# Two gated attentions on one core: the last score group in three parts

## The chip, the cores and the metric

The kernel runs on one core of a Trainium2 chip. The metric is the device time of one execution in microseconds (us), lower is better. Before the change three executions took 889.76, 890.76 and 892.24 us; the median is 890.76. The engines of the core are named as in the profile: PE (TensorE, matrix products), ACT (ScalarE, activation functions), DVE (VectorE), POOL (GpSimd) and SP (SyncE, which here issues DMAs). Scores and sums are accumulated in PSUM, eight banks of 128 x 512 floats.

## The reference

Both branches read the same input of 2048 rows and 640 columns, with 32 heads of 20 columns. Branch A is full softmax attention; branch B looks back over 8 positions with a distance of 2. A sigmoid gate mixes them.

```python
def _A_ref(x, wqkv, wo):                       # B, S, D = 1, 2048, 640; H = 32; Dh = 20
    qkv = (x @ wqkv).reshape(B, S, 3, H, Dh).transpose(2, 0, 3, 1, 4)
    q, k, v = qkv[0], qkv[1], qkv[2]
    scores = jnp.einsum("bhqd,bhkd->bhqk", q, k) * Dh ** -0.5
    p = _softmax(scores, axis=-1)
    o = jnp.einsum("bhqk,bhkd->bhqd", p, v)
    return o.transpose(0, 2, 1, 3).reshape(B, S, D) @ wo
# _B_ref: the same with keys and values of positions s, s-2, ..., s-14 only
g = _sigmoid((x * gate_w).sum(-1, keepdims=True))
return g * _A_ref(x, A_wqkv, A_wo) + (1 - g) * _B_ref(x, B_wqkv, B_wo)
```

## The kernel before, in words

**Groups and units.** Branch A's scores are cut into 32 groups: a chunk of 512 queries (`qc`, four of them) and a quad of four heads (`q`, eight of them), in the order of the list `GO` (line 37). A unit is one head j of the quad and one block of 128 keys against the 512 queries: a product of 128 x 512 scores, 64 units to a group. `HG` is the number of the last group. Before the change it is already cut in two halves of 256 queries (`GX`, line 41), and a unit of it then holds two key blocks of 256 queries each, so that it still fills one bank with 512 columns. In all there are 2048 units.

**Steps.** The program goes in steps that alternate between three and two units (`ST`, line 289: banks 0 to 2 and banks 3 and 4). In a step, PE computes the scores into the banks (`mk_qk`, lines 1258 and 1261), and ACT takes one exponential over all of them (`mk_exp`, line 1306) into one of six buffers `ebuf`. PE later multiplies these by V (`mk_pv`, line 1337) and adds them up in bank 5 (`OB`), which all groups share. Banks 6 and 7 serve all other products.

**Units on VectorE.** Some units get their exponential from VectorE, in pairs: a first step from PSUM for each (line 1489), then four passes over the pair (lines 1509, 1512, 1515, 1522) that form the exponential by a polynomial, into a buffer `xo`. Such a unit uses bank 6 or 7 (`gen_xm`), or takes the third bank of a three-unit step (`xstep`), whose exponential on ACT then covers two units. `xpick` chooses the group; `XMIN`, `XLAST` and `XAHEAD` say how much of a group must still be left, and `X0` is the first step from which it is allowed.

**Normalization.** When a group's products with V are complete, `gen_norm` lets VectorE transpose bank 5 into `rg` (line 723), take reciprocals of the sums (726), multiply by the gate (728), scale (733) and transpose back into `oTn` (736). Only when the first transpose has read bank 5 may the next group's products go there.

**The output.** For the first three chunks `gen_fold` multiplies both branches by their output weights and stores 128-row blocks. For the last chunk, `gen_prefold` does all of branch B and the first five quads (`NPF`) of branch A for its four blocks ahead of time. Blocks 0 and 1 are kept as floats (`accin`, line 803); blocks 2 and 3 as a high and a low bf16 part (`acch`, lines 795 and 798), to be brought back into PSUM by two products with the identity (line 844). After the first half of the last group is normalized (`oTh` 0), `gen_lfold` adds the last three quads of blocks 0 and 1 and stores them from SP, beside the exponentials. For blocks 2 and 3, `gen_l3` and `last_pre2` put the stored parts and two of the last quads into four banks, and `last_end` adds the last quad (four matmuls), copies block 3 on VectorE (line 885) and block 2 on ACT (line 883), and stores each with one DMA (line 815).

**What sets the order.** All instructions are laid down when the program is built. A planner (`_Sched` and the main loop from line 1890) keeps a clock for each engine with fixed costs for each instruction, for exponentials

```python
ED = {3: 1330.0, 2: 903.0, 1: 480.0}
```

in ns for three, two and one unit. Work other than scores stands in lanes, Python generators that offer their next instruction; `turns` ranks them, and `ready` lets one go when its inputs and its engine would be free. Between steps the planner fills PE's time with products with V, with lane work, or with spare products (`spare`) where PE's share of the last 3.4 us would fall under `SPW`. `SEG` (line 1865) gives another set of these parameters for each stretch of 24 steps; stretches that it does not name get `BASE`. The real engines follow the order of their own lists and wait on semaphores for each other.

Of the kernel before, what the change touches and what calls it, by code (L numbers as in the profile page):

```python
# [10 lines left out]
ALU = mybir.AluOpType  # L11
# [3 lines left out]
P = 128  # L15
S = 2048
D = 640
# [23 lines left out]
GX = GO + [(QCN, LQ)]  # L41
GI[(QCN, LQ)] = len(GO)
QL = [n for n, g in enumerate(GO) if n == 0 or GO[n - 1][1] != g[1]]
# [234 lines left out]
def _build(ctx, nc, A_x, A_wqkv, A_wo, B_wqkv, B_wo, gate_w, out):  # L278
# [97 lines left out]
    acch = [qk[:, o * D:(o + 2) * D].rearrange("p (i h k) -> p i h k", i=2, h=2) for o in (4, 6)]  # L376
# [339 lines left out]
    def gen_norm(gi):  # L716
# [3 lines left out]
        n, o = (512, 0) if gi < HG else (256, 256 * (gi - HG))  # L720
# [4 lines left out]
        yield ("dve", 240.0, 0.0)  # L725
        T("dve", lambda e: e.reciprocal(rr[i][:, 0:m], rg[i][:, 0:n:32]), reads=["rg"], writes=[("rr", i)], cost=150.0 + 6 * m)
        yield ("dve", 180.0, 0.0)
# [4 lines left out]
        yield ("dve", 500.0, 0.0)  # L732
        T("dve", lambda e: e.tensor_tensor(rgn[i][:, 0:m, 1:1 + DH], rg_v, rr_b, ALU.mult),
          reads=["rg", ("rr", i)], writes=["rgn"], cost=170.0 + 21 * m)
        yield ("dve", 710.0, 0.0)
        T("dve", lambda e: e.transpose(oTn[:, sl, o:o + n], rgn[i][:, 0:m, :]), reads=["rgn"],
          writes=[("oTn", sl)] if gi < HG else [("oTn", sl), ("oTh", 0)] if gi == HG else [("oTh", 1)], cost=180.0 + n * 1.04)
# [43 lines left out]
    def gen_prefold(qc):  # L781
# [3 lines left out]
        for blk in range(4):  # L785
            for hf in range(2):
# [5 lines left out]
                if blk >= 2:  # L792
                    ac = acch[blk - 2]
                    yield ("dve", 480.0, 0.0)
                    T("dve", lambda e, b=b, hf=hf, ac=ac: e.tensor_copy(ac[:, 0, hf, :], bank[b][:, 0:FW]),
                      reads=[("bk", b)], writes=[("acch", blk, 0, hf), "qB", "kB"], cost=480)
                    yield ("dve", 490.0, 0.0)
                    give(b, T("dve", lambda e, b=b, hf=hf, ac=ac: e.tensor_tensor(ac[:, 1, hf, :], bank[b][:, 0:FW], ac[:, 0, hf, :],
                                                                                 ALU.subtract),
                              reads=[("bk", b), ("acch", blk, 0, hf)], writes=[("acch", blk, 1, hf), "qB", "kB"], cost=490))  # L800
                    continue
# [5 lines left out]
    def a_half(o, blk, hf, qs, rds, first, last, b):  # L807
        for q in qs:
            st, sp = first and q == qs[0], last and q == qs[-1]
            T("pe", lambda e, q=q, st=st, sp=sp: e.matmul(o, *a_mm(o, QCN - 1, q, blk, FW * hf)[1:], start=st, stop=sp),  # L810
              reads=[("oTh", blk // 2) if q == LQ else ("oTn", ((QCN - 1) * NQUAD + q) % NOT)] + [("woA_r", q, j) for j in range(4)],
              **({"writes": [("bk", b)]} if st else {"accum": [("bk", b)]}), cost=140)
# [24 lines left out]
    def l_banks(blk):  # L837
        x = ST[NS_[0] % 2][0]
        return (x, x + 1) if blk == 2 else (6, 7)

    def l_pre(blk, hf, k):
        b = l_banks(blk)[hf]
        if k < 2:
            T("pe", lambda e: e.matmul(bank[b][:, 0:FW], ident[:, :], acch[blk - 2][:, k, hf, :], start=(k == 0), stop=False),
              reads=["ident", ("acch", blk, k, hf)], **({"accum": [("bk", b)]} if k else {"writes": [("bk", b)]}), cost=140)
        else:
            a_half(bank[b][:, 0:FW], blk, hf, [NPF + k - 2], None, False, False, b)

    LP = NQUAD - 1 - NPF + 2

    def gen_l3():
        for hf in range(2):
            while not (pre.done and xmlane.done and normdone.get(HG - 1) and (hf == 0 or lfl.done)):
                yield ("poll",)
            b = yield from take(True, 6 + hf)
            for k in range(LP):
                yield ("pe", 140.0, 1.0)
                l_pre(3, hf, k)
            bst[b] = None
            unch()  # L860

    l2done = [False]

    def last_pre2(s):
        if not l2done[0] and pre.done and normdone.get(HG - 1) and all(x[0] == s - 1 for x in pend):
            l2done[0] = True
            for hf in range(2):
                for k in range(LP):
                    l_pre(2, hf, k)

    def last_end():
        for blk in (3, 2):
            for hf in range(2):
                b = l_banks(blk)[hf]
                a_half(bank[b][:, 0:FW], blk, hf, [LQ], None, False, True, b)
        for blk in (3, 2):
            b = l_banks(blk)[0]
            o_ap = outl[:, blk, :].rearrange("p (h k) -> p h k", h=2)
            i_ap = ps[:, b * 512:(b + 2) * 512].rearrange("p (h k) -> p h k", h=2)[:, :, 0:FW]
            rd = [("bk", b) for b in l_banks(blk)]  # L880
            wr = [("outl", blk, 0), ("outl", blk, 1)]
            if blk == 2:
                T("act", lambda e, o_ap=o_ap, i_ap=i_ap: e.activation(o_ap, i_ap, ACTF.Copy), reads=rd, writes=wr, cost=700)
            else:
                T("dve", lambda e, o_ap=o_ap, i_ap=i_ap: e.tensor_copy(o_ap, i_ap), reads=rd, writes=wr, cost=780)
            out_blk("act" if blk == 2 else "sp", blk)
# [362 lines left out]
    GROUPS = QCN * NQUAD + 1  # L1249
    left = [[GX[g] + (kb, j) for kb in range(KBN if g < HG else KBN // 2) for j in range(4)] for g in range(GROUPS)]  # L1250
    n0 = [len(l) for l in left]

    def qk_mm(e, o, un):
# [5 lines left out]
        h = 256 * (g - HG)  # L1259
        for i in range(2):  # L1260
            ins = e.matmul(o[:, 256 * i:256 * i + 256], kT[js, q, (2 * kb + i) * P:(2 * kb + i + 1) * P], qT[HG % NQT][js, h:h + 256],
                           start=True, stop=True)
# [5 lines left out]
    def kbs(un):  # L1268
        return [un[2]] if GI[un[0:2]] < HG else [2 * un[2], 2 * un[2] + 1]
# [47 lines left out]
    def mk_pv(us):  # L1317
# [10 lines left out]
        def fn(e):  # L1328
            ins = None
            for (key, ap, un), (st, sp) in zip(seq, flags):  # L1330
# [4 lines left out]
                o = 256 * (g - HG) if g >= HG else 0  # L1335
# [23 lines left out]
    def xpick():  # L1359
# [14 lines left out]
    XLAST = 24  # L1374
# [286 lines left out]
    lane(gen_l3(), "l3", gstep(20))  # L1661
# [156 lines left out]
    def turns(s):  # L1818
        act = [g for g in lanes if not g.done and s >= g.s0]
        act.sort(key=lambda g: (not (g.hold or (g.name[:4] == "norm" and int(g.name[4:]) not in obrd)), 0 if g.name == "pre" or g.name[0] == "O" and odl[g.name] - s < ODM else RANK.get(g.name[0], 0), g.dl))  # L1820
# [4 lines left out]
        if xlane.hold and PX:  # L1825
            n = sum(1 for g in act if g.hold or (g.name[:4] == "norm" and int(g.name[4:]) not in obrd))
# [26 lines left out]
    def to(s, t, lim):  # L1853
        while clk["dve"] < t:
# [10 lines left out]
    SEG = {0: (0.68, 150.0, 28, 20, 40, 12, 300000.0, 0, 1000.0, 1, 0.85, 20, 3000.0, 1000000000.0),  # L1865
# [128 lines left out]
```

## Time and profile before

| | |
|---|---|
| median of three executions | 890.76 us |
| the profiled execution: time, span of its instructions | 891.71 us, 889.9 us |
| ACT busy | 873.4 us (98%) |
| VectorE busy, TensorE busy | 821.0 us (92%), 823.0 us (92%) |
| exponentials on ACT | 779 instructions: 338 of three units, 441 of two |
| first exponential starts | 18.52 us |
| mean granted TensorE clock | 0.997 |

In the lines of the groups a row gives the source line, the engine, the operation, the tile written and the tile read, their shapes and the count, then the busy time in us and the mean duration of one in ns, and then the idle time of the engine in front of them with what ended it. Exponentials overlap a little on ACT, so their mean durations add up to more than the busy time. The timeline gives the start, the duration of a merged stretch, and in brackets the idle time ahead of it. The chain is followed back from the last instruction to what released each step. A row by windows gives, for each engine in the order PE, PEld (weight loads), DVE, ACT, POOL, its busy time and its instructions, then the granted TensorE clock, the busy share of the DMA engines and the GB/s that they moved.

### The profile page before, as it was taken

What the parts mean: (1) busy time and instruction counts of PE and PEld (TensorE: products, weight loads), DVE (VectorE), ACT (ScalarE), POOL (GpSimd) and SP (SyncE); (2) the same over time, 40 slices, a digit from 0 to 9 for tenths busy, and PEclk for the clock granted to TensorE, in tenths of its full rate; (3) what the DMA queues carried; (4) which work ended last, traced back from release to release, by engine and by line L of the source; (5) the groups of instructions that cost most, each with busy time, mean ns of one, the idle gap of its engine ahead of it and who ended that gap; (6) DMA issues with size and microseconds to landing.
All of it is one profiled execution on the core that took longest, in us unless ns stands there. A gap on an engine that the chain in (4) does not pass through costs nothing.

```text
span 889.9 us, 16166 instructions
## 1 busy us (share of the span) xinstructions
PE 823.0 (92%) x6702; PEld 257.4 (29%) x6702; DVE 821.0 (92%) x1178; ACT 873.4 (98%) x805; POOL 90.6 (10%) x111
## 2 busy tenths in 40 slices
PE   8999999999999999899998899999998999988897
PEld 6322332223233222222232222233322223322233
DVE  6499999999999999998889999999999999999995
ACT  6999999999999999999999999999999999999996
POOL 2000000000000012210001132001222000232100
PEclk9999999999999999999999999999999999999999
DMA  7232102011111447562113488204466300676300
GB/s 180 42 70 44 13 3 31 1 9 7 14 13 14 90 76 117 94 111 39 17 13 55 79 151 142 32 9 74 81 95 105 53 9 12 106 108 107 58 1 31
DMA packets 141005, 51.27 MB, mean 58 GB/s; under 512 B 120452, under 2 KB 128644, under 8 KB 140932
## 3 DMA queue, kind: packets, MB, share of 16 engines
q0 software_dynamic: 13824, 31.46, 20.9%
q1 hardware_dynamic: 126308, 18.51, 13.6%
q8 instruction: 53, 0.87, 0.4%
q10 hardware_dynamic: 800, 0.27, 0.1%
q14 instruction: 20, 0.16, 0.1%
HBM read 16.14 MB, written 2.62 MB: 21 GB/s over the span
## 4 chain that ended last, share of the span: by engine, by line
ACT 93%; PE 2%; DVE 2%; DMA 1%; issue 1%; SPq 0%; POOL 0%; DVEq 0%
ACT ebuf L1306 93%; DMA xT<-xT 1%; DMA x_tm<-in_A_x_dram 1%; PE ps L1169 0%; ACT L_sb L1037 0%; PE ps L1145 0%; DVE xI L1489 0%; PE ps L1258 0%; DVE xT L1102 0%; DVE xo L1522 0%; DVE xH L1515 0%; PE ps L1337 0%; PE ps L1791 0%; DVE xT L1092 0%; PE ps L469 0%
## 5 line engine op out<-in xcount | busy, mean ns | idle before, releaser
L1306 ACT ACTIVATE ebuf<-ps 128x1024 bf16<-128x1024 f32 (+1 forms) x779 | 860.3, 1468 | 2.0 <-PE ps L1258 1.9
L1258 PE MATMUL ps<-qT,kT 32*128 32x512 bf16 x1984 | 305.0, 385 | 55.7 <-ACT ebuf L1306 47.4
L1337 PE MATMUL ps<-ebuf,vA 128*21 128x512 bf16 (+1 forms) x1952 | 181.9, 377 | 0.9 <-ACT ebuf L1306 0.4
L1258 PEld LDWEIGHTS ps<-qT,kT 32*128 32x128 bf16 x1984 | 74.6, 91 | 345.4 <-ACT ebuf L1306 313.9
L1489 DVE TENSOR_SCALAR xI<-ps 128x512 int32<-128x512 f32 x152 | 103.3, 685 | 21.7 <-PE ps L1258 18.0
L1522 DVE SCALAR_TENSOR_TENSOR xo<-xI,xH 128x1024 int16<-128x1024 int32 x76 | 92.5, 1217 | 0.6
L1512 DVE SCALAR_TENSOR_TENSOR xH<-xU 128x1024 f32<-128x1024 f32 x76 | 92.3, 1215 | 0.6
L1515 DVE SCALAR_TENSOR_TENSOR xH<-xH,xU 128x1024 f32<-128x1024 f32 x76 | 92.1, 1212 | 0.3
L1104 POOL DMA_DIRECT2D accW<-tmps x36 | 31.7, 975 | 576.0 <-DVE tmps L1102 544.5
L469 PE MATMUL ps<-xT,WqkB 128*128 128x512 bf16 x200 | 59.1, 383 | 0.8 <-DVE xI L1489 0.4
L1337 PEld LDWEIGHTS ps<-ebuf,vA 128*21 128x21 bf16 x1952 | 37.0, 90 | 64.1 <-issue 56.4
L1509 DVE TENSOR_SCALAR xU<-xI 128x1024 f32<-128x1024 uint16 x76 | 51.9, 682 | 0.6
L975 DVE TENSOR_TENSOR prod<-qk 128x1024 bf16<-128x1024 bf16 x80 | 52.3, 682 | 0.1
L469 PE MATMUL ps<-xT,WqP 128*128 128x512 bf16 x155 | 47.2, 385 | 0.5 <-DVE qk L938 0.5
L469 PE MATMUL ps<-woA_r,oTn 128*128 128x320 bf16 x232 | 45.0, 301 | 0.0
L469 PE MATMUL ps<-xT,accW 128*128 128x512 bf16 x140 | 42.3, 384 | 0.0
L1791 PE MATMUL ps<-xT,ident 128*128 128x512 bf16 x132 | 41.0, 388 | 0.8 <-DVE xI L1489 0.6
L1796 PE MATMUL ps<-ident,zt 128*128 128x512 bf16 x126 | 41.6, 385 | 0.0
L1102 DVE TENSOR_TENSOR tmps<-vB,attnT 128x1280 f32<-128x1280 bf16 x24 | 35.5, 1479 | 2.4 <-DMA accW<-tmps 2.3
L1102 DVE TENSOR_TENSOR xT<-vB,attnT 128x1280 f32<-128x1280 bf16 x24 | 35.5, 1480 | 1.1 <-DMA xT<-xT 1.1
L678 DVE TENSOR_SCALAR qT<-ps 128x512 bf16<-128x512 f32 x32 | 22.1, 690 | 11.1 <-PE ps L675 10.5
L469 PE MATMUL ps<-WvA,oBacc 128*128 128x320 bf16 x160 | 31.8, 302 | 0.0
(125 smaller groups left out, 718.4 us busy)
## 6 DMA issues: line engine op xcount, KB each, us to landing
accW<-tmps POOLq DMA_DIRECT2D x36, 320.0 KB, 4.2
accW<-xT POOLq DMA_DIRECT2D x24, 320.0 KB, 4.1
xT<-xT POOLq DMA_DIRECT2D x24, 320.0 KB, 4.4
WqkB<-in_B_wqkv_dram SPq DMA_DIRECT2D x40, 160.0 KB
xT<-tmps POOLq DMA_DIRECT2D x12, 320.0 KB, 4.4
WqP<-in_A_wqkv_dram SPq DMA_DIRECT2D x135, 20.0 KB
x_tm<-in_A_x_dram SPq DMA_DIRECT2D x8, 320.0 KB
out_dram<-outsb SPq DMA_DIRECT2D x24, 80.0 KB
```

The source lines that it names most:

```text
L469: ins = e.matmul(o, l, r, start=(k0 + k == 0), stop=(k0 + k == n - 1))
L975: t = T("dve", lambda e, r=r, q_ap=q_ap, k_ap=k_ap: e.tensor_tensor(prod[r][:, :, :], q_ap, k_ap, ALU.mult), reads=["qB", "kB"], writes=[( ...
L1102: T("dve", lambda e, vv=vv, av=av, m=m: e.tensor_tensor(tmp4[m], vv, av, ALU.mult), reads=["aT", "vB4"], writes=[("tmps", m)] + dead, cost ...
L1258: return e.matmul(o, kT[js, q, kb * P:(kb + 1) * P], qT[g % NQT][js, :], start=True, stop=True)
L1306: return T("act", lambda e: e.activation(ebuf[s % NEB][:, 0:512 * n], ps[:, b0 * 512:(b0 + n) * 512], ACTF.Exp, scale=LN2 / ONE), reads=[( ...
L1337: ins = e.matmul(bank[OB][32 * j:32 * j + DH + 1, o:o + w], vA[:, q, kb, VW * j:VW * j + DH + 1], ap[:, w * i:w * i + w], start=st and i = ...
L1489: r = T("dve", lambda e, b=b, i=i, sl=sl: e.tensor_scalar(xIb[sl][:, 512 * i:512 * i + 512].bitcast(I32), bank[b], XB, 0.0, op0=ALU.add, o ...
L1509: T("dve", lambda e, xi=xi: e.tensor_scalar(xU[:, :], xi[:, :].bitcast(U16)[:, 0:2048:2], XV[0], XV[1], op0=ALU.mult, op1=ALU.add), reads= ...
L1512: T("dve", lambda e: e.scalar_tensor_tensor(xH[:, :], xU[:, :], XC[0], xU[:, :], ALU.add, ALU.mult), reads=["xU"], writes=["xH"], cost=1220)
L1515: T("dve", lambda e: e.scalar_tensor_tensor(xH[:, :], xH[:, :], XC[1], xU[:, :], ALU.add, ALU.mult), reads=["xU"], writes=["xH"], cost=1220)
L1522: t = T("dve", lambda e, r=r, xi=xi: e.scalar_tensor_tensor(xo[r][:, :].bitcast(I16), xi[:, :].bitcast(I32), XC[2], xH[:, :], ALU.mult, AL ...
L1796: T("pe", lambda e: e.matmul(bank[OB], zt[:, :], ones4, start=False, stop=False, skip_group_check=True), reads=["ident", "zt"], accum=[("o ...
```

## The change

The last group is cut into parts of 256, 128 and 128 queries (`SUB`), so that there are 34 parts in place of 33. A unit of the two small parts holds four key blocks of 128 queries. The normalizations of these last parts run without a break on VectorE and come ahead of other lanes. Block 2 of the last chunk is now treated as blocks 0 and 1 were: kept as floats, completed by `gen_lfold` once the second part is normalized, and stored from SP beside the exponentials. Only block 3 is left for the end: its stored parts are put into the two banks of the step that would come next, and `last_end` adds the last quad with two matmuls, copies one half on ACT and the other on VectorE, and stores each half with a DMA of its own. The lane `gen_l3` is gone. `XLAST` now counts the units left in all the remaining parts, and is 32 where it was 24. `X0` becomes one of the parameters of a stretch, and the whole table `SEG` is new, so the order of the work changes everywhere behind the prologue. VectorE is given 152 units.

```diff
-GX = GO + [(QCN, LQ)]
+SUB = ((0, 256), (256, 128), (384, 128))
+GX = GO + [(QCN + i, LQ) for i in range(2)]
...
-        n, o = (512, 0) if gi < HG else (256, 256 * (gi - HG))
+        o, n = (0, 512) if gi < HG else SUB[gi - HG]
...
-                if blk >= 2:
-                    ac = acch[blk - 2]
+                if blk == 3:
...
     def gen_lfold():
-        for blk in (0, 1):
+        for blk in (0, 1, 2):
             for hf in range(2):
-                while not (normdone.get(HG) and (blk, hf) in preblk):
+                while not (normdone.get(HG + max(0, blk - 1)) and (blk, hf) in preblk):
...
+    def last_pre2(end):
+        while l2done[0] < 2 and pre.done and normdone.get(HG - 1) and (end or (
+                clk["pe"] >= E[NS_[0] - 2].fin and clk["pe"] + 160.0 * LP < E[NS_[0] - 1].fin)):
+            for k in range(LP):
+                l_pre(l2done[0], k)
+            l2done[0] += 1
+
+    def last_end():
         for hf in range(2):
...
+            b = l_banks()[hf]
+            a_half(bank[b][:, 0:FW], 3, hf, [LQ], None, False, True, b)
+        for hf in range(2):
+            b = l_banks()[hf]
+            o_ap = outl[:, 3, FW * hf:FW * hf + FW]
+            i_ap = bank[b][:, 0:FW]
+            if hf == 0:
+                T("act", lambda e, o_ap=o_ap, i_ap=i_ap: e.activation(o_ap, i_ap, ACTF.Copy), reads=[("bk", b)],
+                  writes=[("outl", 3, hf)], cost=450)
             else:
...
+                T("dve", lambda e, o_ap=o_ap, i_ap=i_ap: e.tensor_copy(o_ap, i_ap), reads=[("bk", b)],
+                  writes=[("outl", 3, hf)], cost=480)
+            T("act" if hf == 0 else "sp", lambda e, o_ap=o_ap, hf=hf: e.dma_start(
+                out_v[:, 4 * (QCN - 1) + 3, FW * hf:FW * hf + FW], o_ap),
+                reads=[("outl", 3, hf)], writes=[("outd", QCN - 1, 3, hf)], dma=True)
...
-        h = 256 * (g - HG)
-        for i in range(2):
-            ins = e.matmul(o[:, 256 * i:256 * i + 256], kT[js, q, (2 * kb + i) * P:(2 * kb + i + 1) * P], qT[HG % NQT][js, h:h + 256],
-                           start=True, stop=True)
+        h, w = SUB[g - HG]
+        for i, k in enumerate(kbs(un)):
+            ins = e.matmul(o[:, w * i:w * i + w], kT[js, q, k * P:(k + 1) * P], qT[HG % NQT][js, h:h + w], start=True, stop=True)
...
-            if g >= GROUPS or len(left[g]) < ((XLAST if g == GROUPS - 1 else XMIN) if g == hg else n0[g] - XAHEAD):
+            if g >= GROUPS or (sum(len(l) for l in left[hg:]) < XLAST if g > HG else len(left[g]) < (XMIN if g == hg else n0[g] - XAHEAD)):
...
-    XLAST = 24
+    XLAST = 32
...
-    SEG = {0: (0.68, 150.0, 28, 20, 40, 12, 300000.0, 0, 1000.0, 1, 0.85, 20, 3000.0, 1000000000.0),
+    SEG = {0: (0.7, 150.0, 28, 20, 40, 11, 300000.0, 0, 500.0, 1, 1.0, 20, 6, 600.0, 1000000000.0),
...
-    BASE = (SPW, XMARG, XMIN, XAHEAD, HOT, GRP, LW, XBO, PVT, PX, LIMF, ODM, XB_[0], XLAG)
+    BASE = (SPW, XMARG, XMIN, XAHEAD, HOT, GRP, LW, XBO, PVT, PX, LIMF, ODM, X0, XB_[0], XLAG)
```

More of the change, by code (lines that the diff above doesn't have):

```diff
@@ L810, in a_half @@
             T("pe", lambda e, q=q, st=st, sp=sp: e.matmul(o, *a_mm(o, QCN - 1, q, blk, FW * hf)[1:], start=st, stop=sp),
-              reads=[("oTh", blk // 2) if q == LQ else ("oTn", ((QCN - 1) * NQUAD + q) % NOT)] + [("woA_r", q, j) for j in range(4)],
+              reads=[("oTh", max(0, blk - 1)) if q == LQ else ("oTn", ((QCN - 1) * NQUAD + q) % NOT)] + [("woA_r", q, j) for j in range(4)],
               **({"writes": [("bk", b)]} if st else {"accum": [("bk", b)]}), cost=140)
@@ L835, in gen_lfold, with l_banks, l_pre @@
             out_blk("sp", blk)
-    def l_banks(blk):
+    def l_banks():
         x = ST[NS_[0] % 2][0]
-        return (x, x + 1) if blk == 2 else (6, 7)
-    def l_pre(blk, hf, k):
-        b = l_banks(blk)[hf]
+        return (x, x + 1)
+    def l_pre(hf, k):
+        b = l_banks()[hf]
         if k < 2:
-            T("pe", lambda e: e.matmul(bank[b][:, 0:FW], ident[:, :], acch[blk - 2][:, k, hf, :], start=(k == 0), stop=False),
-              reads=["ident", ("acch", blk, k, hf)], **({"accum": [("bk", b)]} if k else {"writes": [("bk", b)]}), cost=140)
+            T("pe", lambda e: e.matmul(bank[b][:, 0:FW], ident[:, :], acch[:, k, hf, :], start=(k == 0), stop=False),
+              reads=["ident", ("acch", k, hf)], **({"accum": [("bk", b)]} if k else {"writes": [("bk", b)]}), cost=140)
@@ L846, in l_pre @@
         else:
-            a_half(bank[b][:, 0:FW], blk, hf, [NPF + k - 2], None, False, False, b)
+            a_half(bank[b][:, 0:FW], 3, hf, [NPF + k - 2], None, False, False, b)
     LP = NQUAD - 1 - NPF + 2
-    def gen_l3():
-        for hf in range(2):
[L853 to L883, printed above, removed]
-            else:
-                T("dve", lambda e, o_ap=o_ap, i_ap=i_ap: e.tensor_copy(o_ap, i_ap), reads=rd, writes=wr, cost=780)
-            out_blk("act" if blk == 2 else "sp", blk)
+    l2done = [0]
@@ L1246, in _build @@
     del sch.flow[:]
-    GROUPS = QCN * NQUAD + 1
-    left = [[GX[g] + (kb, j) for kb in range(KBN if g < HG else KBN // 2) for j in range(4)] for g in range(GROUPS)]
+    GROUPS = len(GX)
+    left = [[GX[g] + (kb, j) for kb in range(KBN if g < HG else KBN * SUB[g - HG][1] // 512) for j in range(4)] for g in range(GROUPS)]
     n0 = [len(l) for l in left]
@@ L1268, in kbs @@
     def kbs(un):
-        return [un[2]] if GI[un[0:2]] < HG else [2 * un[2], 2 * un[2] + 1]
+        g = GI[un[0:2]]
+        m = 1 if g < HG else 512 // SUB[g - HG][1]
+        return [m * un[2] + i for i in range(m)]
     head = [0]
@@ L1660, in _build @@
     lfl = lane(gen_lfold(), "lf", gstep(20))
-    lane(gen_l3(), "l3", gstep(20))
     pend = []
@@ L1819, in turns @@
         act = [g for g in lanes if not g.done and s >= g.s0]
-        act.sort(key=lambda g: (not (g.hold or (g.name[:4] == "norm" and int(g.name[4:]) not in obrd)), 0 if g.name == "pre" or g.name[0] == "O" and odl[g.name] - s < ODM else RANK.get(g.name[0], 0), g.dl))
+        act.sort(key=lambda g: (not (g.hold or (g.name[:4] == "norm" and (int(g.name[4:]) not in obrd or int(g.name[4:]) >= HG))), 0 if g.name == "pre" or g.name[0] == "O" and odl[g.name] - s < ODM else RANK.get(g.name[0], 0), g.dl))
         if xsp[0] is not None:
@@ L1825, in turns @@
         if xlane.hold and PX:
-            n = sum(1 for g in act if g.hold or (g.name[:4] == "norm" and int(g.name[4:]) not in obrd))
+            n = sum(1 for g in act if g.hold or (g.name[:4] == "norm" and (int(g.name[4:]) not in obrd or int(g.name[4:]) >= HG)))
             return act[:n] + [xrlane] + act[n:] + [xmlane, xlane]
@@ L1947, in _build @@
             force(g, NS)
-    last_pre2(NS)
+    last_pre2(True)
     for g in list(lanes):
```

34 lines of the change are left out of this document (20 added, 14 removed), and 42 rows, old and new, of the table SEG.

## The prediction

> **What bounds the kernel now.** I read the page's busy shares and the chain first, then the groups with shapes kept apart.
>
> ```profile
> PE 823.0 (92%) x6702; PEld 257.4 (29%) x6702; DVE 821.0 (92%) x1178; ACT 873.4 (98%) x805; POOL 90.6 (10%) x111
> ACT 93%; PE 2%; DVE 2%; DMA 1%; issue 1%; SPq 0%; POOL 0%; DVEq 0%
> ```
>
> ```profile
> L1306 ACT ACTIVATE ebuf<-ps 128x1536 bf16<-128x1536 f32 x338 | 577.1, 1707 | 1.4 <-PE ps L1258 1.3
> L1306 ACT ACTIVATE ebuf<-ps 128x1024 bf16<-128x1024 f32 x441 | 527.6, 1284 | 0.6 <-PE ps L1258 0.6
> ...
> L1489 DVE TENSOR_SCALAR xI<-ps 128x512 int32<-128x512 f32 x152 | 103.3, 685 | 21.7 <-PE ps L1258 18.0 <-PE ps L1261 2.3
> ```
>
> ScalarE (ACT) is the bound: 93% of the chain is its exponentials. They hold 338 x 3 + 441 x 2 = 1896 units of 128x512 scores; VectorE does the other 152 of 2048. ACT idles 2.0 us before all 779 exponentials together, so it cannot be fed better by more than that. The timeline of ACT shows where it idled after the start, and when its last exponential ends:
>
> ```profile
> 804.39 1.45 ACT L1306 ACTIVATE ebuf<-ps 128x1536 bf16<-128x1536 f32 x1 [0.53 <-PE ps L1258]
> 806.42 75.83 ACT L1306 ACTIVATE ebuf<-ps 128x1024 bf16<-128x1024 f32 x68 [0.58 <-PE ps L1258]
> ```
>
> 806.42 + 75.83 = 882.25. So the time is the part up to the first exponential (its code is not changed), the exponentials, and 889.9 - 882.25 = 7.65 us behind the last of them. The chain of waits shows the work in these last 7.65 us:
>
> ```profile
> 882.31 0.63 PE ps L1337 x8
> ...
> 882.96 0.46 DVE rg L723
> ...
> 883.88 0.34 DVE rgn L733
> ...
> 884.24 0.46 DVE oTn L736
> ...
> 884.75 0.73 PE ps L810 x4
> ...
> 885.50 0.70 ACT WvB L883
> ```
>
> After that comes the store. The profiled execution took 891.71 us (span 889.9 and 1.8 around it), 0.95 above the median of 890.76; I work out differences and take them off the median.
>
> **The change part by part.**
>
> *The normalization behind the last exponential.* It handles 128 queries where it handled 256. The rows for 512 and 256 give the slope:
>
> ```profile
> L723 DVE STREAM_TRANSPOSE rg<-ps 128x512 f32<-128x512 f32 x31 | 22.0, 709 | 0.2
> L736 DVE STREAM_TRANSPOSE oTn<-rgn 128x512 bf16<-128x512 bf16 x31 | 21.8, 704 | 0.1
> L733 DVE TENSOR_TENSOR rgn<-rg,rr 128x320 bf16<-128x320 f32 x31 | 15.1, 487 | 0.1
> ...
> L723 DVE STREAM_TRANSPOSE rg<-ps 128x256 f32<-128x256 f32 x2 | 0.9, 446 | 0.5 <-PE ps L1337 0.5
> L736 DVE STREAM_TRANSPOSE oTn<-rgn 128x256 bf16<-128x256 bf16 x2 | 0.9, 442 | 0.0
> ...
> L733 DVE TENSOR_TENSOR rgn<-rg,rr 128x160 bf16<-128x160 f32 x2 | 0.6, 324 | 0.0
> ```
>
> First transpose: (709 - 446)/256 = 1.03 ns a query, so 128 fewer save 0.13 us. Second: (704 - 442)/256 = 1.02 ns, again 0.13 us. Multiplication: (487 - 324)/256 = 0.64 ns, 0.08 us. The two small ones between them stay. Sum -0.34 us, all on the chain.
>
> *The last product, copy and store.* Two matmuls, of one block, replace four of two blocks; each half is copied and stored by itself (ACT the first, VectorE the second).
>
> ```profile
> L803 DVE COPY qk<-ps 128x320 f32<-128x320 f32 x4 | 1.9, 482 | 0.0
> L1175 ACT ACTIVATE kT<-ps,e 128x256 bf16<-128x256 f32 x8 | 3.8, 474 | 2.0 <-DVE Kmax L1173 1.8
> L883 ACT ACTIVATE WvB<-ps 128x640 bf16<-128x640 f32 x1 | 0.7, 704 | 3.2 <-PE ps L810 3.2
> L810 PE MATMUL ps<-woA_r,oTn 128*128 128x320 bf16 x24 | 4.8, 301 | 0.1
> ```
>
> ```profile
> 883.14 0.43 PE L810 MATMUL ps<-woA_r,oTn 128*128 128x320 bf16 x2
> ```
>
> Before: 0.73 for four matmuls, 0.02 between, 0.70 for the copy: 1.45 us. After, by ACT: 0.30 for one matmul, 0.02, and a copy of 320 columns; between the rows of 256 (0.474) and 640 (0.704) this is 0.51: 0.83 us. By VectorE: 0.43 for two, 0.02, 0.48: 0.93 us. The later one counts: -0.52 us. The data of the last two stores, 320 KB, moved here:
>
> ```profile
> 886.75:887.00 0.25, 0.00 (x0) 0.00 (x0) 0.00 (x0) 0.00 (x0) 0.00 (x0) 1.00 0.27 92
> 887.00:887.25 0.25, 0.00 (x0) 0.00 (x0) 0.00 (x0) 0.00 (x0) 0.00 (x0) 1.00 1.03 364
> ...
> 888.00:888.25 0.25, 0.00 (x0) 0.00 (x0) 0.00 (x0) 0.00 (x0) 0.00 (x0) 0.94 0.08 33
> ```
>
> They run from about 886.9 to 888.05. 160 KB less at 364 GB/s is 0.44 us. The bounds are no gain (if what follows the last byte, 1.8 us of the span, hides it) and 0.6 (half of the 1.15 us); I take -0.4, near the rate that the row shows.
>
> *The last batch of products with V.* Today it is 8 matmuls in 0.63 us. The last group has 16 units and batches of ten are wanted, so six units may be left, each of four narrow matmuls: 24. The rows below show 16 in 0.63 and their weight loads in 0.34, so 24 may cost up to 24/16 x 0.34 - 0.34 = 0.17 more. I take +0.1, with 0 to 0.2. The sum behind the last exponential is -0.34 - 0.52 - 0.4 + 0.1 = **-1.2 us**, between -0.6 and -1.5.
>
> *Narrower matmuls in the last two groups, and work moved ahead of the end.* The last 256 queries take 32 units. At four matmuls of 128 a unit they issue 128 score and 128 value matmuls in place of 64 and 64.
>
> ```profile
> 880.80 0.34 PEld L1337 LDWEIGHTS ps<-ebuf,vA 128*21 128x21 bf16 x16 [0.21 <-issue]
> 880.80 0.63 PE L1337 MATMUL ps<-ebuf,vA 128*21 128x256 bf16 x16
> ```
>
> ```profile
> 860.00:882.30 22.30, 20.63 (x269) 9.23 (x268) 17.10 (x31) 22.26 (x21) 0.00 (x0) 1.00 0.03 9
> ```
>
> A load takes 0.34/16 = 21 ns and hides the shorter matmul, so the 128 added ones cost 2.7 us of TensorE; the six matmuls of block 2 that move ahead add 6 x 0.15 = 0.9. The window shows TensorE idle for 1.7 of 22.3 us: at worst 1.9 us are uncovered, at best none, since a busy TensorE is not one at its peak. I take 0: the cover is what TensorE waits for each exponential. If it is gone, exponentials start late. VectorE idles 5.2 us in this window: the third normalization (about 1.2 us) and the two additions of block 2 (0.49 each) lie there; the two halves of block 2 are no longer split in a high and a low part, which offsets the plain copies that replace them. Running a short normalization without a break, and first, delays at most one exponential chain of VectorE by 1.2 us. Block 2's store goes to SP's queue, which holds only the two before it; POOL's queue gets nothing. The block-3 products with the earlier groups (eight matmuls, 1.2 us) move under the last exponential or beside the final normalization, where 16 of them ran before: 0.
>
> *The order anew.* 152 units on VectorE are what it has now, so ACT keeps 1896. What can differ is how many three-unit steps lend a bank to VectorE (now (441 - 338 + 1)/2 = 52), and whether TensorE or VectorE is late. Each lent bank makes 0.4 more exponentials. The fixed part of one is small: from
>
> ```profile
> L1306 ACT ACTIVATE ebuf<-ps 128x1536 bf16<-128x1536 f32 x91 | 157.0, 1725 | 0.0
> L1306 ACT ACTIVATE ebuf<-ps 128x1024 bf16<-128x1024 f32 x126 | 149.7, 1295 | 0.0
> ```
>
> ```profile
> 227.54 238.16 ACT L1306 ACTIVATE ebuf<-ps 128x1024 bf16<-128x1024 f32 x217
> ```
>
> 217 exponentials with 525 units in 238.16 us; at the 0.427 us a unit of the code's own cost table (an estimate: 1330 - 903 ns) 14 us, or 0.06 us each, are fixed. A lent bank costs 0.024 us; all 52 gone or twice as many is -1.2 or +1.2 us. I take 0. X0 now lets VectorE start at step 6 and no longer 25, in the first stretch, which loads it earlier and the rest less. For lateness, the one stall of before is the price:
>
> ```profile
> 800.73 0.10 PEld L1258 LDWEIGHTS ps<-qT,kT 32*128 32x128 bf16 x3 [1.25 <-ACT ebuf L1306]
> ```
>
> ```profile
> 800.00:801.00 1.00, 0.26 (x3) 0.10 (x3) 1.00 (x2) 1.00 (x2) 0.00 (x0) 1.00 0.97 169
> ...
> 803.00:804.00 1.00, 1.00 (x5) 0.10 (x3) 0.97 (x2) 0.86 (x1) 0.46 (x1) 0.50 1.06 192
> ...
> 805.00:806.00 1.00, 1.00 (x4) 0.21 (x3) 1.00 (x2) 0.84 (x1) 0.00 (x0) 0.50 1.12 202
> ```
>
> TensorE was busy 0.26 of 800 to 801; by 803 its granted clock was 0.50, and the two exponentials behind it waited 0.53 + 0.58 = 1.11 us. A dip costs 1.1 us, and where it falls depends on the order. I take as many as now: one.
>
> The Trainium skill, "TensorE: Matmul & The Clock Gate" (section "Why this matters for your kernels"), has it that the clock is kept as long as gaps between matmuls stay under about 3 us. Here it fell with a longest wait of 1.25 us, so the row decides; by the page no order of this kind would dip, and the sum would stand at -1.2 with the first rival at nothing.
>
> **The rivals.**
>
> *A: more clock dips (slower).* Place: stretches where TensorE has only the score matmuls, as at 800. Price 1.11 us each. It decides from 893.43 (890.76 x 1.003), that is 889.6 + 3.9: four added dips, 894.0; five, 895.1. For it: the order is wholly new, and 5.2 us of idle ACT in 864 would suffice. Against it: one dip in the whole span now.
>
> *B: TensorE binds in the last two groups (slower).* If the narrow matmuls did not overlap, each would cost its columns in a full array: four of 320 take 0.73 and two 0.43, so 0.15 each, 0.06 for 128. 256 x 0.06 + 26 x 0.15 (the products with the output weights) = 19.3 us against 32 x 0.4556 = 14.6 of ACT (863.73 us / 1896 units): +4.7, so 894.3. It binds above (14.6 - 3.9)/256 = 42 ns a matmul; the row of 16 in 0.63 gives 39 with its tail, the loads 21.
> The same page of the Trainium skill (section "Back-to-back issue gap") states about 81 ns for a sustained 128-column pair; by it the sum would be an estimated 20.7 + 3.9 - 14.6 = +10 us. The row of 39 ns speaks against it.
>
> *C: the new order is also cleaner (faster).* The dip goes (-1.1) and half the lent banks (-0.6): 889.6 - 1.7 = 887.9. For it: VectorE starts its share earlier; against it: 1.1 us is all that ACT has left to lose inside the stream.
>
> *D: the end is not shortened (no change).* The output bank is shared: the last group's value products wait until VectorE has read the group before it, whose units may include late VectorE ones. What is gained behind the last exponential would be lost in front of it: 890.8.
>
> **How the numbers follow.** Forecast 0.50, at 890.76 - 1.2 = 889.6 us, by itself 888.3 to 891.5 (the tail's bounds, one dip more or less, the lent banks). A 0.25, B 0.04, C 0.14, D 0.07. A difference of 0.3% (2.7 us) is about what a measurement of this kernel can tell from none. The forecast and D lie within it: 0.57. C is faster: 0.14. A and B are slower: 0.29. The range of 887.4 to 894.8 takes in C's centre and A up to four dips; beyond it lie about 0.12 of A and B above and 0.04 of C below.
>
> **What would show it.** Two exponential shapes that still add up to 1896 units, and about 152 first steps on VectorE; behind the last exponential about 6.4 us in place of 7.65, with transposes near 0.31 us, two last matmuls in 0.43 and copies near 0.5; a granted clock of 0.99 or more with at most two stretches at 0.50. The prediction is wrong if ACT idles over 4 us before exponentials (A, with the clock at 0.50 beside it; B, if in the last 15 us), or if another number of units is on ACT.

## The result, and the profile after

The changed kernel takes 889.29 us (median of 21 executions, 888.98 to 890.24); the kernel before took 890.68 in the same comparison (21 executions, 889.66 to 895.55). The ratio is 0.998, with a 95% interval of 0.9974 to 0.9987: a small gain, within the 0.3% that I called no change, and 0.3 us from the forecast of 889.6. The profiled execution of the changed kernel took 889.44 us with a span of 887.6.

Busy shares and the chain by engine, from the page of the changed kernel:

```profile
PE 807.9 (91%) x6718; PEld 259.0 (29%) x6807; DVE 823.3 (93%) x1183; ACT 873.0 (98%) x807; POOL 90.3 (10%) x111
ACT 96%; PE 2%; DVE 0%; DMA 0%; issue 0%
```

The groups with shapes kept apart, also of the changed kernel:

```profile
L1301 ACT ACTIVATE ebuf<-ps 128x1536 bf16<-128x1536 f32 x335 | 574.6, 1715 | 1.1 <-PE ps L1252 0.8 <-PE ps L1255 0.3
L1301 ACT ACTIVATE ebuf<-ps 128x1024 bf16<-128x1024 f32 x445 | 533.3, 1292 | 0.0
...
L1484 DVE TENSOR_SCALAR xI<-ps 128x512 int32<-128x512 f32 x152 | 103.9, 686 | 23.7 <-PE ps L1252 20.7 <-PE ps L1255 1.7
```

335 x 3 + 445 x 2 = 1895 units, and the very last exponential has one more: 1896, as before, with 152 on VectorE. The last rows of ACT's timeline:

```profile
744.30 127.16 ACT L1301 ACTIVATE ebuf<-ps 128x1024 bf16<-128x1024 f32 x115
871.79 9.63 ACT L1301 ACTIVATE ebuf<-ps 128x1536 bf16<-128x1536 f32 x9 [0.33 <-PE ps L1255]
883.66 0.44 ACT L873 ACTIVATE WvB<-ps 128x320 bf16<-128x320 f32 x1 [2.24 <-PE ps L815]
```

The two waits near 805 are gone; a new one of 0.33 us stands at 871.79. The last exponential ends at 871.79 + 9.63 = 881.42. The chain at the end, followed back from the last instruction, names ACT up to 877.77 and from there on runs along TensorE's list:

```profile
870.55 0.46 DVE oTn L742
...
871.05 0.31 PE ps L815
871.36 0.41 PE ps L1255 x12
...
871.79 5.98 ACT ebuf L1301 x5
...
881.05 0.83 PE ps L1332 x32
...
881.91 0.33 DVE rg L725
...
882.67 0.26 DVE rgn L738
...
882.95 0.32 DVE oTn L742
...
883.31 0.46 PE ps L815 x2
...
883.80 0.49 DVE WvB L876
```

Of the 32 matmuls at 881.05, the last four need the last exponential: in the trace they start from 881.48, 0.05 us behind its end.

The two profiled executions differ by 2.3 us of span (887.64 to two places after the change), in two parts:

| part, us | before | after | difference |
|---|---|---|---|
| up to the first exponential | 18.52 | 18.54 | +0.02 |
| exponentials | 863.73 | 862.88 | -0.85 |
| behind the last exponential | 7.65 | 6.22 | -1.43 |

The difference of the medians is only 1.39. The experiments show why: the profiled execution of before has a clock dip that most of its executions do not have, and the change also loses something in front of the end.

### The profile page after: what moved, and what is told of

It is laid out like the page before. It is cut to its first block, busy times and chain, and to the rows that moved or that the text cites. A ratio compares the mean times of both kernels' runs of the same rounds, so it can differ in the third digit from the quotient of the medians.

```text
span 887.6 us, 16302 instructions
## 1 busy us (share of the span) xinstructions
PE 807.9 (91%) x6718; PEld 259.0 (29%) x6807; DVE 823.3 (93%) x1183; ACT 873.0 (98%) x807; POOL 90.3 (10%) x111
## 4 chain that ended last, share of the span: by engine, by line
ACT 96%; PE 2%; DVE 0%; DMA 0%; issue 0%
ACT ebuf L1301 96%; PE ps L1139 1%; PE ps L1163 1%; ACT L_sb L1031 0%; DMA x_tm<-in_A_x_dram 0%; PE ps L1255 0%; PE ps L1332 0%; PE ps L815 0%; PE ps L577 0%; PE ps L1180 0%; PE ps L471 0%; DVE rg L725 0%; DVE oTn L742 0%; DVE qT L680 0%; DVE rgn L738 0%
## 5 line engine op out<-in xcount | busy, mean ns | idle before, releaser
L1301 ACT ACTIVATE ebuf<-ps 128x1024 bf16<-128x1024 f32 (+2 forms) x781 | 860.4, 1473 | 1.1 <-PE ps L1252 0.8
L1332 PE MATMUL ps<-ebuf,vA 128*21 128x512 bf16 (+2 forms) x2014 | 186.4, 370 | 0.0
L1332 PEld LDWEIGHTS ps<-ebuf,vA 128*21 128x21 bf16 x2014 | 39.5, 90 | 64.9 <-issue 54.1
L471 PE MATMUL ps<-xT,WqkB 128*128 128x512 bf16 x185 | 55.5, 383 | 2.0 <-issue 1.7
L471 PE MATMUL ps<-woA_r,oTn 128*128 128x320 bf16 x232 | 47.0, 302 | 0.0
L471 PE MATMUL ps<-xT,WqP 128*128 128x512 bf16 x140 | 43.1, 383 | 1.5 <-issue 1.3
L1785 PE MATMUL ps<-xT,ident 128*128 128x512 bf16 x118 | 36.8, 384 | 1.1 <-issue 1.1
L471 PE MATMUL ps<-xT,accW 128*128 128x512 bf16 x119 | 36.1, 383 | 1.9 <-issue 1.1
L1790 PE MATMUL ps<-ident,zt 128*128 128x512 bf16 x107 | 35.6, 385 | 0.3 <-issue 0.3
L1332 PE MATMUL ps<-xo,vA 128*21 128x512 bf16 (+2 forms) x162 | 30.7, 372 | 0.0
```

Source lines behind the costliest of these rows:

```text
L471: ins = e.matmul(o, l, r, start=(k0 + k == 0), stop=(k0 + k == n - 1))
L1301: return T("act", lambda e: e.activation(ebuf[s % NEB][:, 0:512 * n], ps[:, b0 * 512:(b0 + n) * 512], ACTF.Exp, scale=LN2 / ONE), reads=[( ...
L1332: ins = e.matmul(bank[OB][32 * j:32 * j + DH + 1, o:o + w], vA[:, q, kb, VW * j:VW * j + DH + 1], ap[:, w * i:w * i + w], start=st and i = ...
L1785: T("pe", lambda e, b=b: e.matmul(bank[b], ident[:, :], xT[:, 3, 0, :], start=True, stop=True), reads=["ident", ("xT", 3)], accum=[("bk", ...
```

## The experiments

**Does the gain come from the new end or from the new order?** Two kernels exchange the halves. The first has the changed code with the old table:

```diff
-    SEG = {0: (0.7, 150.0, 28, 20, 40, 11, 300000.0, 0, 500.0, 1, 1.0, 20, 6, 600.0, 1000000000.0),
+    SEG = {0: (0.68, 150.0, 28, 20, 40, 12, 300000.0, 0, 1000.0, 1, 0.85, 20, 25, 3000.0, 1000000000.0),
...
```

> The changed code with the parameter table of before (X0 25 throughout). It puts 150 units on VectorE and 1898 on ScalarE, two more than both kernels, which at 0.4556 us a unit costs 0.9 us. My theory (the gain is the shorter end, about -1.5 us in the profile, and the rest is one clock dip more or less): about 6.2 us behind the last exponential and 890.68 - 1.4 + 0.9 = 890.2 us, up to 891.3 with one more dip at a granted clock of 0.50. The rival (the gain is the new order's, the end gives nothing): 890.7 + 0.9 = 891.6 us.

Measured: 890.21 us (12 executions), a ratio of 0.9998 (0.9988 to 1.0008) to the kernel before. But no execution lies near that median. Six have a mean granted clock of 0.999 or more and take 889.08 to 889.42 us; six have 0.996 or 0.997 and take 890.99 to 892.48. The profiled one is of the second kind; its ACT timeline ends so:

```profile
804.56 1.45 ACT L1301 ACTIVATE ebuf<-ps 128x1536 bf16<-128x1536 f32 x1 [0.60 <-PE ps L1252]
806.52 76.84 ACT L1301 ACTIVATE ebuf<-ps 128x1024 bf16<-128x1024 f32 x69 [0.51 <-PE ps L1252]
```

It has the dip of before at the same place. Its last exponential ends at 883.36 of a span of 889.4: 6.0 us behind it, near the 6.2 of the changed kernel. So the shorter end is the changed code's, whatever the table. And the dip is not in every execution of one and the same program. That the median falls on the 890.2 I had expected is chance, since it lies between two clusters.

Like is compared with like in the executions without a dip: their median is 889.32 here and 890.05 in the 18 of before that went with this run (clock 0.999 or more). That is 0.73 less with two more units on ACT, which cost 0.91: under the old table the new end is worth 1.6 us, and the profile has 7.65 - 6.02 = 1.63. By the same estimate the changed kernel, at 889.29 with two units fewer than this one, loses about 0.9 us to the new table in such executions. What the new table brings is that no execution dips.

The second kernel has the old code with the new table:

```diff
-    SEG = {0: (0.68, 150.0, 28, 20, 40, 12, 300000.0, 0, 1000.0, 1, 0.85, 20, 3000.0, 1000000000.0),
+    SEG = {0: (0.7, 150.0, 28, 20, 40, 11, 300000.0, 0, 500.0, 1, 1.0, 20, 6, 600.0, 1000000000.0),
...
-    BASE = (SPW, XMARG, XMIN, XAHEAD, HOT, GRP, LW, XBO, PVT, PX, LIMF, ODM, XB_[0], XLAG)
+    BASE = (SPW, XMARG, XMIN, XAHEAD, HOT, GRP, LW, XBO, PVT, PX, LIMF, ODM, X0, XB_[0], XLAG)
```

> The kernel before with the new parameter table and X0 as one of its parameters. It puts 154 units on VectorE and 1894 on ScalarE, two fewer, -0.9 us. My theory: 7.6 us behind the last exponential, and 890.68 - 0.9 = 889.8 us, or 0.6 lower if the new order has no dip. The rival (the gain is the order's): 889.29 - 0.9 = 888.4 us.

Measured: 891.26 us (11 executions), 1.0005 (0.9996 to 1.0014). All eleven executions have a clock of 0.999 or more, so the new order has no dip with the old end either. Neither of the two times came out. The rows of ACT say why:

```profile
744.03 135.77 ACT L1306 ACTIVATE ebuf<-ps 128x1024 bf16<-128x1024 f32 x123
884.91 0.70 ACT L883 ACTIVATE WvB<-ps 128x640 bf16<-128x640 f32 x1 [5.11 <-PE ps L810]
```

The exponentials end at 879.80, earlier than in any other kernel, since two units fewer are on ACT. But 9.5 us follow. In this order two additions of the first two blocks (0.91 us on VectorE) come behind the last exponential and ahead of the first transpose. The sixteen products that prepare the last two blocks come behind it in the kernel before too, but there they start 0.6 us after it (882.86) and run beside the normalization. Here they wait for the additions until 881.98, 2.2 us after it, and stand in the chain. The old end with the new table is a pair that nobody planned; the run shows the absence of dips, and not the worth of the order.

**Is the dip what costs the time?** In the kernel before, the score matmuls of steps 704 to 710 are issued twice, the second time with the same values:

```diff
-            for i, un in enumerate(us):
-                ins = qk_mm(e, bank[b0 + i], un)
+            for r in range(2 if 704 <= s <= 710 else 1):
+                for i, un in enumerate(us):
+                    ins = qk_mm(e, bank[b0 + i], un)
```

> The kernel before, with the score matmuls of steps 704 to 710 issued twice (the second writes the same values); the order is otherwise the same. It adds about 7 x 0.2 us to TensorE just where its clock fell. If the dip is what made ScalarE wait 0.53 + 0.58 us: no stretch at 0.50 near 800, no wait of ScalarE there, and a time about 0.5 to 1.1 us below that of before (889.6 to 890.2). If the dip is without effect on the time, or comes from elsewhere: 890.7, and the waits stay.

Measured: 890.84 us (11 executions, 890.24 to 891.21), 1.0002 (0.9993 to 1.0011). All eleven have a clock of 0.998 or more, and there is no stretch at 0.50 near 800. The dip is gone and the time did not fall, because the doubled matmuls themselves made exponentials late. In step 706 the second set of scores starts 0.23 us behind the first (799.10 for 798.87 in the trace), and the exponential at 799.52 waited for it by 0.22:

```profile
799.52 4.62 ACT L1307 ACTIVATE ebuf<-ps 128x1536 bf16<-128x1536 f32 x4 [0.22 <-PE ps L1258]
804.38 77.01 ACT L1307 ACTIVATE ebuf<-ps 128x1536 bf16<-128x1536 f32 x69 [0.23 <-PE ps L1258]
```

The last exponential ends at 881.39 against 882.25 in the dipped profile of before: 0.86 us earlier, with two waits of 0.22 and 0.23 in place of 0.53 and 0.58. The time is that of neither kind of execution of before. What the dip is worth is read from those themselves. Of the 33 executions of the kernel before that went with the next runs, 23 have a clock of 0.999 or more and take 889.64 to 890.74 us, median 890.10; ten have 0.997 or less and take 891.83 to 893.30, median 891.92. (In the two other comparisons of the experiments 10 of 29 and 5 of 14 executions of it had 0.997 or less.) **A dip costs 1.8 us**, and not the 1.11 us that ACT shows as idle. The rest is overlap. An exponential starts before the one ahead of it has left the pipeline. The starts and durations (ns, from the trace of before) around the dip, with the usual distance of starts (1347 after three units, 912 after two):

```
start    duration  units   to the next start   usual   late
801402   1540      3       1331                1347
802733   1126      2       1659                 912    +747
804392   1451      3       2031                1347    +684
806423   1024      2       1085                 912    +173
```

747 + 684 + 173 = 1604 ns, where the idle time counts 533 + 580. The profile thus shows 1.6 of the 1.8 us. What idle time leaves out is the overlap that the wait has used up.

**What makes the clock fall?** In the changed kernel the 245 spare matmuls keep their place and their planned cost, but have 16 columns in place of 512:

```diff
-                T("pe", lambda e, b=b: e.matmul(bank[b], ident[:, :], xT[:, 3, 0, :], start=True, stop=True),
+                T("pe", lambda e, b=b: e.matmul(bank[b][:, 0:16], ident[:, :], xT[:, 3, 0, 0:16], start=True, stop=True),
```

(and the same in the other three branches of `spare`).

> The changed kernel in the same order, with its 245 spare matmuls cut from 512 to 16 columns, so that TensorE loses about 90 us of busy time and no wait is added. My theory (the clock falls with a low busy share, without any long gap, and each dip costs ScalarE about 1.1 us): five to twenty stretches at 0.50 and 895 to 911 us. The rule of the Trainium skill that only gaps above about 3 us let the clock fall: no dip, 889.3 us.

Measured: 914.12 us (910.26 to 914.60), 1.0256 (1.0238 to 1.0274), a mean clock of 0.926, twelve separate stretches at 0.50 before the end of the work, some four to eight windows long. The time is 3 us above my upper figure of 911. The longest wait of a matmul in it, in the rows of waits:

```profile
PE ps L1252 <- ACT ebuf L1301: 70.6, 192, 0.8
```

The last figure is the longest single wait: 0.8 us (1.1 for a weight load). So the clock falls without any long gap. The window ahead of the first fall, the fall itself, and the return:

```profile
327.01:330.43 3.42, 2.52 (x28) 0.89 (x28) 3.26 (x5) 3.42 (x5) 0.00 (x0) 1.00 0.00 0
330.43:333.84 3.41, 2.34 (x23) 0.73 (x21) 3.41 (x5) 3.41 (x4) 0.00 (x0) 1.00 0.00 0
333.84:337.25 3.41, 3.31 (x28) 0.86 (x31) 3.41 (x4) 3.33 (x5) 1.75 (x2) 0.50 0.57 99
347.49:350.91 3.42, 3.25 (x30) 1.01 (x31) 2.38 (x4) 2.96 (x3) 0.00 (x0) 1.00 0.70 111
```

Second column: length; third: TensorE's busy time; the figure ahead of the last two: the granted clock. After a window of 3.41 us with 2.34 us busy (69%) the next has 0.50. In the kernel before it was the same:

```profile
799.47:802.89 3.42, 2.18 (x20) 0.59 (x19) 3.39 (x5) 3.42 (x4) 0.92 (x2) 1.00 0.99 175
802.89:806.30 3.41, 3.41 (x14) 0.45 (x12) 3.38 (x4) 2.42 (x3) 0.87 (x2) 0.50 0.98 175
```

64% busy in one window, and exactly the next one at half clock. In these traces every stretch at 0.50 inside the work lasts one such window or several (one to eight). The windows that were followed by a fall had 57 to 76% (the modelled busy share), those that were not had 66% or more; the bound lies somewhere in that overlap.

The Trainium skill, "TensorE: Matmul & The Clock Gate" (section "What's actually happening"), states a free-running window of 3413 ns, and that the phase differs between executions. The length agrees with the rows, 3.41 us, and the phase is the likeliest reason why a fixed program dips in some executions only; I could not set the phase, so this stays argued, but the traces support it. Shift the window along the trace of before:

```profile
797.90:801.31 3.41, 2.39 (x27) 0.69 (x20) 3.38 (x4) 3.41 (x4) 1.63 (x2) 1.00 0.65 114
798.90:802.31 3.41, 2.11 (x19) 0.53 (x18) 3.38 (x4) 3.41 (x4) 1.28 (x2) 1.00 0.97 173
```

Up to the fall at 802.89, only windows that end behind 801.8 us have less than 66% (the rows show 70 and 62%). That is 1.1 us of 3.41, so about three phases in ten meet such a window, and ten of 33 executions dipped. In the trace of the changed kernel no phase meets a window under 66%, and none of 21 executions dipped.

The section "Why this matters for your kernels" of the same page of the Trainium skill names gaps of over about 3 us as what costs the clock. Here 0.8 us was the longest wait of a matmul, and 25 us were lost: keeping the gaps short was not enough.

**Where do the terms of the end come from?** One store of the whole last block, from SP:

```diff
-            T("act" if hf == 0 else "sp", lambda e, o_ap=o_ap, hf=hf: e.dma_start(
-                out_v[:, 4 * (QCN - 1) + 3, FW * hf:FW * hf + FW], o_ap),
-                reads=[("outl", 3, hf)], writes=[("outd", QCN - 1, 3, hf)], dma=True)
+        out_blk("sp", 3)
```

> The changed kernel with one store of the whole last block, from SP, after both copies. The later copy sets the start as now, so I expect 0 to +0.2 us behind the last exponential (6.17 to 6.4 us in the profile). If two queues with half the data each were what shortened the end: about +0.5 us (6.7 us).

Measured: 889.38 us (10 executions), 0.9983 (0.9974 to 0.9992) to the kernel before. Span 887.4, last exponential at 881.11: 6.34 us behind it, +0.12. Two stores in place of one are worth about that, no more.

Block 2's store held back to the end:

```diff
-            out_blk("sp", blk)
+            if blk < 2:
+                out_blk("sp", blk)
...
+            if hf == 0:
+                T("sp", lambda e: e.dma_start(out_v[:, 4 * (QCN - 1) + 2, :], outl[:, 2, :]),
+                  reads=[("outl", 2, h) for h in range(2)] + [("outl", 3, 0)], writes=[("outd", QCN - 1, 2)], dma=True)
```

> The changed kernel with block 2's store held back until ACT's last copy is done, so that 320 KB instead of 160 KB move behind the end; its issue puts 0.13 us on SP ahead of the last store. If the data set the end, as the prediction's term of -0.4 us has it: +0.4 to +0.6 us behind the last exponential (6.6 to 6.8 us). If the wait for the landing hides the data: +0.13 us at most.

Measured: 889.56 us (10 executions), 0.9991 (0.9982 to 1.0001). Span 888.0, last exponential at 881.38: 6.65 us behind it, +0.43. 160 KB more behind the end cost 0.43 us with 0.14 of it the issue (SP issues its last store at 884.46 in place of 884.32). The data count; the landing does not hide them. In the changed kernel the last 160 KB move here:

```profile
885.00:885.25 0.25, 0.00 (x0) 0.00 (x0) 0.00 (x0) 0.00 (x0) 0.00 (x0) 1.00 0.92 256
885.25:885.50 0.25, 0.00 (x0) 0.00 (x0) 0.00 (x0) 0.00 (x0) 0.00 (x0) 1.00 1.02 308
885.50:885.75 0.25, 0.00 (x0) 0.00 (x0) 0.00 (x0) 0.00 (x0) 0.00 (x0) 1.00 0.28 80
```

**Do narrow matmuls bind TensorE?** Four parts of 128 queries double the narrow part:

```diff
-SUB = ((0, 256), (256, 128), (384, 128))
+SUB = ((0, 128), (128, 128), (256, 128), (384, 128))
...
-      reads=[("oTh", max(0, blk - 1)) if q == LQ
+      reads=[("oTh", blk) if q == LQ
...
```

> The changed kernel with the last group in four parts of 128 queries: 128 more narrow matmuls on TensorE (64 for scores, 64 for values) and one more normalization. My theory (narrow matmuls run side by side at about 21 ns): nothing in the last 30 us becomes later by more than 0.3 us, 889.3 us or, because block 0 is completed earlier, a few tenths less. Rival B (each costs its columns in a full array, 0.06 us, so 7.7 us more of TensorE): exponentials wait for scores in the last 30 us, +3 to +7 us, 892 to 896 us.

Measured: 889.32 us (11 executions), 0.9986 (0.9978 to 0.9995). Rival B falls: ACT's timeline has no wait above 0.2 us in the last 137 us, and the stretch of the last 124 exponentials is shorter than in the changed kernel, where it is 871.79 + 9.63 - 744.30 = 137.12 us:

```profile
744.42 136.96 ACT L1302 ACTIVATE ebuf<-ps 128x1024 bf16<-128x1024 f32 x124
```

What the narrow matmuls cost is seen in the changed kernel's last batch. Its first 28, spread over four column groups of the array, start in 0.43 us (880.99 to 881.41 in the trace), 16 ns apart on average. The last four, all of one group, start 56 to 61 ns apart. So the groups run side by side. The Trainium skill's figure of about 81 ns a pair ("TensorE: Matmul & The Clock Gate", "Back-to-back issue gap") is not for such groups.

**What is the new wait at 871.79?** In the chain above, the last transpose of the 256-query part ends at 871.00, then comes the block-0 matmul that reads it (871.05), and only behind it the scores (871.36) for which the exponential of 871.79 waits. TensorE takes its list in order, so the scores waited for VectorE. In the next two kernels the lane that completes the blocks offers its matmuls only when the values are due (the second reads `("oTh", blk)`, since each of its blocks has its own part):

```diff
+                yield after(sch.bufs[("oTh", max(0, blk - 1))][0])
                 b = yield from take(True)
```

First in three parts, as the changed kernel has them:

> The changed kernel with three parts as it has them, and only the wait of e9: the lane that completes blocks 0 to 2 offers its matmuls when the normalized values are due. If the matmul that waited for VectorE ahead of the scores was the cause of the late exponentials: the one late by 0.54 us near 871.8 is on time, and the stream of exponentials is 0.5 us shorter. Block 2 is completed later in this order, which may cost up to 0.5 us behind the last exponential; 888.8 to 889.3 us. If TensorE's load was the cause: the exponential stays late and the time is 889.3 us or more.

Measured: 889.61 us (11 executions), 0.9989 (0.9980 to 0.9998). The last rows of ACT:

```profile
744.22 136.69 ACT L1302 ACTIVATE ebuf<-ps 128x1024 bf16<-128x1024 f32 x124
884.05 0.44 ACT L874 ACTIVATE WvB<-ps 128x320 bf16<-128x320 f32 x1 [3.15 <-PE ps L815]
```

The time missed the 888.8 to 889.3 that I had expected. The wait is gone and the same 124 exponentials take 136.69 us, 0.43 less. But the last exponential ends at 880.91 of a span of 888.0: 7.1 us follow in place of 6.2. The chain shows what came between:

```profile
881.90 0.49 DVE WvB L838
882.39 0.23 DVE rg L725
```

Block 2 is completed after the last exponential, and its addition stands on VectorE ahead of the last transpose. The gain in front is lost twice over behind.

Then in four parts:

> The same with four parts, and the lane that completes blocks 0 to 2 offers its matmuls only when the normalized values that they read are due. In the changed kernel the score matmuls of one step stood behind such a matmul on TensorE while it waited for VectorE (0.46 us in the chain, two exponentials late by 0.54 and 0.22 us). If that wait is the cause: no exponential in the last 30 us late by over 0.3 us, and 888.5 us. If TensorE's load is the cause: the lateness stays, 889.3 us or more.

Measured: **888.91 us** (11 executions, 888.64 to 889.20), 0.998 (0.9971 to 0.9989) to the kernel before; 0.4 us below the changed kernel; its slowest execution is below that kernel's median. It has both: the stream without the wait, and no addition behind it.

```profile
743.82 136.69 ACT L1303 ACTIVATE ebuf<-ps 128x1024 bf16<-128x1024 f32 x124
882.74 0.44 ACT L875 ACTIVATE WvB<-ps 128x320 bf16<-128x320 f32 x1 [2.23 <-PE ps L816]
```

The last exponential ends at 880.51, and 6.2 us follow. With a block to each part, block 0 is complete sooner, so the lanes that wait have time. I had expected 888.5. The second late exponential, of 0.22 us at 866.76 in the changed kernel, is not this wait's: with the wait removed and the order else unchanged up to there (the three parts above), it is still 0.22 us late, at 866.67.

## Why the prediction was right, point by point

- *Bound.* Right. ACT held 1896 units in both kernels, and nothing but waits and the two ends could change much. But the 2.0 us of idle time was no limit on what better feeding could give: the dip alone held back 1.6 us, of which idle time shows 1.1.
- *Normalization, -0.34.* From the first transpose to the end of the last: 882.96 to 884.70 before, 881.91 to 883.27 after, -0.38. The slopes held.
- *Product and copies, -0.52.* 884.75 to 886.20 before, 883.31 to 884.29 after: 1.45 to 0.98, -0.47. ACT's half took 0.44 and not 0.51; VectorE's half, 0.49, set the end as said.
- *Store, -0.4.* From the end of the last copy to the end of the span 3.70 before and 3.35 after: -0.35. The late store confirms it: 0.43, of which 0.29 are not its issue.
- *Last batch, +0.1.* Wrong in sign. It went from 0.69 (882.25 to 882.94) to 0.46 (881.42 to 881.88), -0.23. The batch had eight units and not six, 32 matmuls; but the last step has one unit, so 28 of them had started while its exponential was still on ACT, and four remained. I had not worked out how many units the last step would have. The end is -1.43 in all, near the edge of the -1.5 I gave.
- *Narrow matmuls and work moved ahead, 0 (at worst 1.9).* The narrow matmuls cost nothing, as the four parts show. The work moved ahead did: "running a short normalization without a break, and first" was costed on VectorE alone. I did not ask who waits for it: a block-0 matmul on TensorE, with scores queued behind. It is worth 0.43 us, by the kernel with the wait removed. Rival D had the loss in front of the end, but named the output bank; it was the order in TensorE's list, so D's mechanism is not shown.
- *The order, "as many dips as now: one".* Wrong twice. The dip of before is in ten of 33 executions, so the profile had drawn the rarer kind. And the changed kernel shows none in 21: all have 0.999 or more. *Price 1.1 us*: it is 1.8, since idle time does not count the overlap lost. From executions without a dip, 890.10 to 889.29 is -0.8. The parts come to about that. Without the 1.60 us of the dip, the exponentials of before would take 863.73 - 1.60 = 862.13 us; in the changed kernel they take 862.88, which is 0.75 more. Two late starts account for it: 0.54 at 871.79 and 0.22 at 866.76, whose cause stays open. -1.43 + 0.75 + 0.02 = -0.66, and the rest is smaller than the spread of either kernel's executions. So the forecast of -1.2 had the end nearly right and missed a loss ahead of it, and the base of 890.76 had part of the dip in it. That 889.6 lies 0.3 us from the measured 889.29 is in part luck.
- *Rivals.* C came in half: the dip went, the lent banks did not fall (55 for 51; of the 52 that I counted, one was the last step, which had only two units left). The 5.2 us of idle time that I named for A reach the upper end of the range; 3.9 were enough for it to decide. A did not come. B is refuted.

## What to carry to other kernels

When work is moved ahead of the end, ask of each instruction what stands behind it in its engine's list; a matmul that waits for VectorE holds back everything after it, scores too. Price a stall of a pipelined engine by the distance of starts, and not by the idle time in the profile. Where the executions of one kernel spread by more than the effect, sort them by granted clock first; a kernel that never dips is worth more than its best time tells.

## What the hardware did that I had not expected

The clock fell with TensorE 64% busy (before) and 69% busy (thin spares) over a window of 3.41 us, with no wait of a matmul above 1.0 and 0.8 us (of a weight load 1.25 and 1.1). The spares, 245 matmuls that compute nothing, are worth 914.12 - 889.29 = 24.8 us here. With four column groups in use, 128-column matmuls started 16 ns apart on average, and 56 to 61 ns apart in a single group.
